# Windowed attention and a mixture of eight experts on one core: attention in steps ordered by shape, experts by 13 prepared widths, first slots of expert 0 beside routing

## The chip, the cores and the metric

The kernel runs on 1 core of a Trainium2 chip. The metric is device time in microseconds. All data are fp32. The engines are TensorE (PE; its weight loads stand apart as PEld), VectorE (DVE), ScalarE (ACT), GpSimd (POOL) and SyncE (SP); DMAs are issued from the queues of SP, ACT and POOL.

## The reference, cut to what matters

```python
# attention: q, k, v (4, 8, 768, 64); n_global = 8, n_local = 96
scores = q @ k.T / 8 - slope[h] * dist       # keep keys < n_global, and 0 <= i - j < n_local
a = softmax(scores);  x = (a @ v), heads side by side     # (3072, 512)
# router: 8 experts, one for each token
logits = (x / |x|) @ (emb / |emb|).T / tau
e = argmax(logits);  gate = softmax(logits)[e]
# expert e: w1[e] (512, 1024), w2[e] (1024, 512)
out[token] = gate * (relu(x[token] @ w1[e]) @ w2[e])
```

How many tokens an expert has depends on the data.

## The kernel before, in words

**Attention** (window_attention, L277). A group is one batch and four heads; there are 8. A group has 8 units (j = 0 to 7) of 96 keys and the first 30 rows as global keys; a unit's queries are the 192 columns from its first key on (96 for the last). For a unit TensorE computes scores (score, L337: four products of 64 rows by 126 by 192 columns), ScalarE takes exp (L341), VectorE multiplies by a table that holds bias and mask (L347), and one unit later TensorE adds the products with v (attend, L367, column pieces of 64) and the row sums (L373, column pieces of 32) in PSUM; a group's fourth and eighth unit close a half, which is copied out (L380, L382). Ahead of that, q and k are turned by transposes through `ident` (turn, L320). For every 128 tokens of a batch there follow: products with the normalised expert vectors `enb` (L405), transposes of the sums (L408) and of those products (L410), transposes of x (L430), a scaling by the reciprocal sum (L432), a store to `x_dram` and a sum of squares (L438).

**Routing** (choose, L145). Per batch, or per half of the last batch, VectorE finds the best expert as a one-hot `oh`; TensorE counts, by a product with the triangle `prefix` and one with `ones` (L171, L172), how many tokens of the same expert come earlier; VectorE adds the running count `cnt` and gets a slot; POOL scatters (token, gate) into that slot of `meta` (L199). Expert e owns slots e*3072 onwards.

**Experts** (load_rows L626, expert L648). For each expert SP reads the first 512 slots, POOL gathers four tiles of 128 rows of x (L640); empty slots point to a zero row. TensorE turns them (L655), VectorE copies (L656); 32 first products with 512 columns (L664), relu on ScalarE (L666); 32 second products, four tiles of 128 slots by 8 (L671); VectorE multiplies by the gate (L674), POOL scatters the rows to the output (L675). Every expert is computed at 512 slots. An unused tail (leftover, L681) handles more than 512 tokens of an expert and unusual n_global, n_local; all engines jump over it.

The order of the work on every engine comes from the framework's scheduler, which follows the order of the code and its priorities; waits between engines are semaphores. Weights alternate between two buffers.

## Time and profile before

| | us |
|---|---|
| median of 3 runs (lowest, highest) | 768.54 (766.0, 772.91) |
| the profiled execution | 777.63 |
| its span, first to last instruction | 775.8 |
| TensorE busy | 686.5 (88% of the span) |
| VectorE, ScalarE, POOL busy | 182.4, 147.6, 112.6 |
| mean granted TensorE clock | 0.95 |

The page has the span in 40 slices of 19.4 us; each digit is the busy share of a slice in tenths. PEclk is the granted clock, where 1.00 is 2.4 GHz and 0.50 is 1.2 GHz. In the chain of waits each step is the work that ended last. Idle time in brackets stands before a row, with what ended it. An fp32 product appears as two instructions in the trace, a transpose as one.

### The profile page before, as it was taken

What the parts mean: (1) busy time and instruction counts of PE and PEld (TensorE: products, weight loads), DVE (VectorE), ACT (ScalarE), POOL (GpSimd) and SP (SyncE); (2) the same over time, 40 slices, a digit from 0 to 9 for tenths busy, and PEclk for the clock granted to TensorE, in tenths of its full rate; (3) what the DMA queues carried; (4) which work ended last, traced back from release to release, by engine and by line L of the source; (5) the groups of instructions that cost most, each with busy time, mean ns of one, the idle gap of its engine ahead of it and who ended that gap; (6) DMA issues with size and microseconds to landing.
All of it is one profiled execution on the core that took longest, in us unless ns stands there. A gap on an engine that the chain in (4) does not pass through costs nothing.

```text
span 775.8 us, 8382 instructions
## 1 busy us (share of the span) xinstructions
PE 686.5 (88%) x3394; PEld 353.0 (46%) x3394; DVE 182.4 (24%) x500; ACT 147.6 (19%) x280; POOL 112.6 (15%) x131
## 2 busy tenths in 40 slices
PE   4989986989799519999999999999999999999992
PEld 2556654555465304444444444444444444444440
DVE  2435562664366601011011011011011011011010
ACT  3545532543453200100100100100100100100100
POOL 2110022013003232012012012012012011010010
PEclk9999989898999758999999999999999999999996
DMA  9977669650110922214214115115114114000000
GB/s 185 213 129 213 177 177 39 137 118 7 37 42 16 283 48 90 83 58 174 81 53 171 78 71 175 71 64 172 64 70 168 64 77 146 0 37 14 0 26 18
DMA packets 99898, 74.57 MB, mean 96 GB/s; under 512 B 80762, under 2 KB 80890, under 8 KB 99850
## 3 DMA queue, kind: packets, MB, share of 16 engines
q1 hardware_dynamic: 90538, 58.44, 29.8%
q0 software_dynamic: 5888, 14.71, 5.4%
q10 hardware_dynamic: 3424, 0.79, 0.6%
q8 instruction: 29, 0.48, 0.3%
q14 instruction: 19, 0.16, 0.1%
HBM read 61.11 MB, written 14.90 MB: 98 GB/s over the span
## 4 chain that ended last, share of the span: by engine, by line
PE 59%; DVE 4%; DMA 3%; issue 0%; POOL 0%; SPq 0%; ACT 0%; DVEq 0%; ACTq 0%
PE big L664 29%; PE work L671 28%; DVE xT L656 2%; DMA x_dram<-xs 1%; DMA xg<-x_dram,ids 1%; DMA meta<-mt,slot 1%; DVE y L674 1%; PE tp L405 0%; PE tp L430 0%; PE tp L408 0%; DMA emt<-meta 0%; PE od L367 0%; PE work L655 0%; POOL out_dram L675 0%; SPq L630 0%
## 5 line engine op out<-in xcount | busy, mean ns | idle before, releaser
L664 PE MATMUL big<-xT,w1t 128*128 128x512 f32 x512 | 224.0, 598 | 11.2 <-DVE xT L656 11.2
L671 PE MATMUL work<-w2t,hT 128*128 128x512 f32 x512 | 221.0, 592 | 0.0
L664 PEld LDWEIGHTS big<-xT,w1t 128*128 128x128 f32 x512 | 97.4, 192 | 133.2 <-issue 120.0
L671 PEld LDWEIGHTS work<-w2t,hT 128*128 128x128 f32 x512 | 97.3, 190 | 122.5 <-issue 122.5
L674 DVE TENSOR_SCALAR y<-work,emt 128x512 f32<-128x512 f32 x32 | 24.0, 751 | 387.2 <-PE work L671 387.2
L666 ACT ACTIVATE hT<-big 128x1024 f32<-128x1024 f32 x32 | 32.8, 1023 | 432.0 <-PE big L664 432.0
L347 DVE TENSOR_TENSOR ex<-ex,table 126x384 f32<-126x384 f32 (+1 forms) x128 | 70.1, 585 | 89.0 <-ACT ex L341 89.0
L675 POOL DMA_INDIRECT out_dram<-y,ids x32 | 31.8, 995 | 337.8 <-DVE y L674 330.1
L337 PE MATMUL sp<-qT,kT 64*126 64x192 f32 (+1 forms) x512 | 66.8, 364 | 7.9 <-ACT qT L325 5.8
L367 PE MATMUL od<-ex,v 126*64 126x192 f32 (+1 forms) x576 | 62.6, 320 | 8.6 <-issue 4.6
L341 ACT ACTIVATE ex<-sp 126x768 f32<-126x768 f32 x64 | 49.1, 767 | 82.6 <-PE sp L337 60.8
L337 PEld LDWEIGHTS sp<-qT,kT 64*126 64x126 f32 x512 | 43.9, 196 | 28.1 <-issue 13.1
L367 PEld LDWEIGHTS od<-ex,v 126*64 126x64 f32 x576 | 34.1, 138 | 28.5 <-issue 18.6
L640 POOL DMA_INDIRECT xg<-x_dram,ids x32 | 30.9, 966 | 85.4 <-issue 42.9
L373 PE MATMUL od<-ex,ones 126*32 126x192 f32 (+1 forms) x576 | 36.3, 321 | 0.0
L655 PE MATMUL work<-ident,xg 128*128 128x128 f32 x128 | 17.7, 293 | 18.9 <-DMA xg<-x_dram,ids 18.9
L199 POOL DMA_INDIRECT meta<-mt,slot x24 | 23.8, 993 | 44.1 <-DVE slot L190 30.3
L655 PEld LDWEIGHTS work<-ident,xg 128*128 128x128 f32 x128 | 15.5, 151 | 23.7 <-DMA xg<-x_dram,ids 20.1
L320 PE MATMUL tp<-ident,k 128*128 128x128 f32 x96 | 19.7, 329 | 6.3 <-DMA k<-in_k_dram 6.0
L311 POOL COPY v<-v 30x1792 f32<-30x1792 f32 x8 | 13.6, 1698 | 74.8 <-DMA v<-in_v_dram 46.6
L430 PE MATMUL tp<-ident,xd 128*128 128x128 f32 x96 | 16.3, 298 | 8.2 <-DVE lh L420 6.3
L656 DVE COPY xT<-work 128x512 f32<-128x512 f32 x32 | 20.1, 682 | 6.8 <-PE work L655 6.5
(113 smaller groups left out, 297.4 us busy)
## 6 DMA issues: line engine op xcount, KB each, us to landing
w1t<-in_moe_w_dram SPq DMA_DIRECT2D x8, 2048.0 KB, 7.9
w2t<-in_moe_w_dram SPq DMA_DIRECT2D x8, 2048.0 KB, 10.8
k<-in_k_dram SPq DMA_DIRECT2D x32, 192.0 KB, 3.5
v<-in_v_dram SPq DMA_DIRECT2D x32, 192.0 KB, 4.5
x_dram<-xs SPq DMA_DIRECT2D x24, 256.0 KB, 6.3
q<-in_q_dram SPq DMA_DIRECT2D x28, 192.0 KB, 3.9
q<-in_q_dram ACTq DMA_DIRECT2D x4, 192.0 KB, 6.1
xg<-x_dram,ids POOLq DMA_INDIRECT x32
```

The costliest lines, as they stand in the source:

```text
L337: nc.tensor.matmul(sp[0:ROWS, e, a * n : (a + 1) * n], lhsT=t.kT[rows, j, 0:ROWS], rhs=t.qT[rows, j * BLK : j * BLK + n], start=True, stop ...
L341: nc.scalar.activation(ex, sp[0:ROWS, :, 0 : 2 * n], AF.Exp, scale=k.scale)
L347: nc.vector.tensor_tensor(out=exv, in0=exv, in1=tb, op=ALU.mult)
L367: nc.tensor.matmul(od[a][e * D : (e + 1) * D, cols], lhsT=g.v[0:ROWS, 2 * a + e, j, :], rhs=ex[:, e, a * n + c0 : a * n + c1], start=first ...
L373: nc.tensor.matmul(od[2][32 * i : 32 * i + 32, cols], lhsT=k.ones[0:ROWS, 0:32], rhs=ex[:, e, a * n + c0 : a * n + c1], start=first, stop= ...
L655: nc.tensor.transpose(ps[:, c, :], xgs[j][:, c * P : (c + 1) * P], k.ident[:])
L656: nc.vector.tensor_copy(out=xT[:, :, j * P : (j + 1) * P], in_=ps[:])
L664: nc.tensor.matmul(ps[:, i, :], lhsT=w1[:, c, f * P : (f + 1) * P], rhs=xT[:, c, :], start=c == 0, stop=c == k.NC - 1)
L666: nc.scalar.activation(hT[:, 2 * f2 : 2 * f2 + 2, :], ps[:], AF.Relu)
L671: nc.tensor.matmul(ps[:], lhsT=hT[:, f, j * P : (j + 1) * P], rhs=w2[:, f, :], start=f == 0, stop=f == k.NF - 1)
L674: nc.vector.tensor_scalar_mul(y[:], ps[:], mt[:, j, 1:2])
L675: nc.gpsimd.indirect_dma_start(out=k.out[:, :], out_offset=bass.IndirectOffsetOnAxis(ap=ids[:, j : j + 1], axis=0), in_=y[:], in_offset=No ...
```

## The change

Attention now runs in 32 steps of two units (a fourth of a group); inside a step all scores come first, then transposes, then the products with v and the row sums of the step before. Exp is taken for one head parity at a time, the table is applied once for a unit. Sums of both groups of a batch share one tile (`halves`), so one transpose does for two. The choice is split into pieces that stand in later steps. The code's order is kept by `manual_schedule` on TensorE, ScalarE, VectorE and SP. The global rows of v come by DMA for every unit, not by a copy on POOL. Weights of expert 0 and 1 come in 32 pieces each, one at a time between other loads, both during the attention.

The last batch's halves are run so that its first half is routed early. After three batches the first 256 slots of expert 0 are gathered (first_rows), and their first products stand on TensorE around the last choice (first_product); the rest of expert 0 starts at the slot behind.

For every expert a width among 128, 160, ..., 512 is picked from its count (choose_widths). TensorE and ScalarE, and they alone, read it into a register (take_width) and jump into one of 13 prepared arms (Switch) that holds first products with that many columns, the next expert's transposes, second products of the full tiles but the first, and a remainder of 64 and 32 slots computed in two or four column pieces of the output (part_in_arm). The first tile's second products follow outside the arm (second). Each arm ends with a jump to the common end. A hint for the jump into the arm stands where the width is read, one for the jump out at the arm's start. Outputs of tiles that an arm doesn't compute have ids beyond the last row, which the scatter drops.

```diff
 CAP = 512
+PIECES = 32
+FIRST = 256
+WIDTHS = [128] + list(range(160, CAP + 1, 32))
...
-    nc.tensor.matmul(cp[:, 0:w], lhsT=k.prefix[:], rhs=ohf, start=True, stop=True)
-    nc.tensor.matmul(cp[:, w : 2 * w], lhsT=k.ones[:], rhs=ohf, start=True, stop=True)
+    nc.tensor.matmul(cp[:, 0:w], lhsT=k.prefix[:], rhs=oh.rearrange("p t e -> p (t e)"), start=True, stop=True,
+                     skip_group_check=True)
+    for t in range(n):
+        nc.tensor.matmul(cp[:, (t + 1) * E : w + E], lhsT=k.ones[:],
+                         rhs=oh[:, t : t + 1, :].to_broadcast([P, n - t, E]), start=False, stop=True,
+                         skip_group_check=True)
...
+    nc.vector.tensor_tensor(out=both, in0=cp[:, 0 : w + E].rearrange("p (t e) -> p t e", e=E),
+                            in1=k.cnt[:].unsqueeze(1).broadcast_to([P, n + 1, E]), op=ALU.add)
+    nc.vector.tensor_copy(out=k.cnt[:], in_=both[:, n, :])
...
         j, n = u.j, u.n
-        sp = sp_p.tile([P, 2, 512], F32, name="sp", tag="sp")
+        u.sp = [bank() for _ in range(2)]
+        u.ex = (late_p if u.late else ex_p).tile([P, 2, 2, 2 * BLK], F32, name="ex", tag="ex")
+        u.ex = u.ex[0:ROWS, :, :, 0:n]
         for a in range(2):
             t = u.g.pairs[a]
             for e in range(2):
                 rows = slice(e * D, (e + 1) * D)
-                nc.tensor.matmul(sp[0:ROWS, e, a * n : (a + 1) * n], lhsT=t.kT[rows, j, 0:ROWS],
+                nc.tensor.matmul(u.sp[e][0:ROWS, a * n : (a + 1) * n], lhsT=t.kT[rows, j, 0:ROWS],
                                  rhs=t.qT[rows, j * BLK : j * BLK + n], start=True, stop=True)
-        nc.scalar.activation(ex, sp[0:ROWS, :, 0 : 2 * n], AF.Exp, scale=k.scale)
-        kind = min(j, 2)
...
+    def grow(u, e):
+        nc.scalar.activation(u.ex[:, e], u.sp[e][0:ROWS, 0 : 2 * u.n].rearrange("p (a c) -> p a c", a=2), AF.Exp,
+                             scale=k.scale)
+    def weigh(u):
+        kind = min(u.j, 2)
+        tab = k.table[0:ROWS, u.g.m].rearrange("p e a i c -> p (e a) i c")[:, :, kind::(3 - kind), :]
+        exv = u.ex.rearrange("p e a (i c) -> p (e a) i c", c=BLK)
+        nc.vector.tensor_tensor(out=exv, in0=exv, in1=tab[:, :, 0 : u.n // BLK, :], op=ALU.mult)
...
+    def attend(g, p):
+        if p % 2 == 0:
+            g.od = [po_p.tile([P, 512], F32, name="od%d" % i, tag="od%d" % i) for i in range(3)]
+        parts = []
+        if p == 2:
+            parts.append((g.units[3], 0, BLK, 2 * BLK, True))
+        for j in (2 * p, 2 * p + 1):
+            parts.append((g.units[j], (j % QB) * BLK, 0, BLK if j % QB == QB - 1 else 2 * BLK, j == 0))
+        for u, at, c0, c1, first in parts:
             for a in range(2):
                 for e in range(2):
-                    nc.tensor.matmul(od[a][e * D : (e + 1) * D, cols], lhsT=g.v[0:ROWS, 2 * a + e, j, :],
-                                     rhs=ex[:, e, a * n + c0 : a * n + c1], start=first, stop=True,
+                    nc.tensor.matmul(g.od[a][e * D : (e + 1) * D, at : at + c1 - c0],
+                                     lhsT=g.v[0:ROWS, 2 * a + e, u.j, :],
+                                     rhs=u.ex[:, e, a, c0:c1], start=first, stop=True,
                                      skip_group_check=True)
+        for u, at, c0, c1, first in parts:
             for a in range(2):
                 for e in range(2):
                     i = 2 * a + e
-                    nc.tensor.matmul(od[2][32 * i : 32 * i + 32, cols], lhsT=k.ones[0:ROWS, 0:32],
-                                     rhs=ex[:, e, a * n + c0 : a * n + c1], start=first, stop=True,
+                    nc.tensor.matmul(g.od[2][32 * i : 32 * i + 32, at : at + c1 - c0], lhsT=k.halves[0:ROWS, g.m].rearrange("p i c -> p (i c)"),
+                                     rhs=u.ex[:, e, a, c0:c1], start=first, stop=True,
                                      skip_group_check=True)
...
+    def first_product(f):
+        if f % 2 == 0:
+            k.first.ps = bank()
+        ps = k.first.ps
+        for c in range(k.NC):
+            nc.tensor.matmul(ps[:, (f % 2) * FIRST : (f % 2 + 1) * FIRST], lhsT=k.w[0][0][:, c, f * P : (f + 1) * P],
+                             rhs=k.first.xT[:, c, :], start=c == 0, stop=c == k.NC - 1)
+        if f % 2:
+            nc.scalar.activation(k.first.hT[:, f - 1 : f + 1, :], ps[:].rearrange("p (i n) -> p i n", i=2), AF.Relu)
...
+        us = g.units[2 * p : 2 * p + 2]
+        for u in us:
             score(u)
-            if gi + 1 < len(groups):
-                turn(groups[gi + 1].pairs[u.j // 4], u.j % 4)
+        grow(us[0], 0)
+        grow(us[0], 1)
+        if s == 0:
+            next(table)
+        weigh(us[0])
+        grow(us[1], 0)
...
+        todo = [(x.pairs[a], i) for x, a, i in turns[s]]
+        if todo:
+            turn(*todo.pop(0))
+        grow(us[1], 1)
+        for x in todo:
+            turn(*x)
...
+        for hf in active:
+            half_turns(hf)
+        if s < len(steps) - 2:
+            weigh(us[1])
+        weights_part()
+        if s > 0:
+            q, qp = steps[s - 1]
+            attend(q, qp)
+            if q.m == 1 and qp % 2:
...
+    attend(*steps[-1])
+    for hf in active:
+        half_turns(hf)
+        half_router(hf)
+    hf = start_half(t, 1)
+    score_experts(hf, bank())
+    first_turn()
+    turn_sums(hf)
+    xs = [turn_x(t, 3)]
+    turn_products(hf)
+    next(hf.router)
+    xs += [turn_x(t, 4), turn_x(t, 5)]
+    for i in range(3):
+        store_x(t, 3 + i, xs[i])
+    weights_part(len(weights))
+    first_product(0)
+    hf.router.send(bank())
+    next(hf.router)
+    next(hf.router)
+    check_sums(t)
+    first_product(1)
+    for f in range(2, k.NF):
+        first_product(f)
...
+def turn_row(k, rows, xT, j, copy):
+    ps = k.work.tile([P, k.NC, P], F32, name="work", tag="work")
+    for c in range(k.NC):
+        k.nc.tensor.transpose(ps[:, c, :], rows[2][j][:, c * P : (c + 1) * P], k.ident[:])
+    copy(out=xT[:, :, j * P : (j + 1) * P], in_=ps[:])
...
+def second_in_arm(k, t, hT, w2, j):
+    nc = k.nc
+    ps = k.work.tile([P, k.DM], F32, name="work", tag="work")
+    for f in range(k.NF):
+        nc.tensor.matmul(ps[:], lhsT=hT[:, f, j * P : (j + 1) * P], rhs=w2[:, f, :],
+                         start=f == 0, stop=f == k.NF - 1)
+    nc.scalar.mul(t.y[:, j, :], ps[:], t.rows[0][:, j, 2:3])
+def part_in_arm(k, t, hT, w2, base, size):
+    nc, n = k.nc, P // size
+    m = k.DM // n
+    ps = k.work.tile([P, k.DM], F32, name="work", tag="work")
+    for f in range(k.NF):
+        for i in range(n):
+            nc.tensor.matmul(ps[i * size : (i + 1) * size, 0:m], lhsT=hT[:, f, base : base + size],
+                             rhs=w2[:, f, i * m : (i + 1) * m], start=f == 0, stop=f == k.NF - 1)
+    nc.scalar.mul(t.y_part[size][:], ps[:, 0:m], t.parts[size][1][:])
...
+def first_by_eight(k, xT, w1, hT, w, between=None):
+    nc = k.nc
+    for f in range(k.NF):
+        ps = k.big.tile([P, CAP], F32, name="big", tag="big")
         for c in range(k.NC):
+            nc.tensor.matmul(ps[:, 0:w], lhsT=w1[:, c, f * P : (f + 1) * P], rhs=xT[:, c, 0:w],
+                             start=c == 0, stop=c == k.NC - 1)
+        nc.scalar.activation(hT[:, f, 0:w], ps[:, 0:w], AF.Relu)
+        if between:
+            between(f)
...
+    if coming:
+        coming.xT = k.xtp.tile([P, k.NC, CAP], F32, name="xT", tag="xT")
+    def between(f):
+        for j in {5: (0,), 6: (1, 2), 7: (3,)}.get(f, ()) if coming else ():
+            turn_row(k, coming.rows, coming.xT, j, k.nc.scalar.copy)
+    tiles = range(0 if behind else 1, CAP // P)
+    for arm in tc.Switch(now.width.index, len(WIDTHS), hint=now.width.hint):
+        w = WIDTHS[arm]
+        first_by_eight(k, now.xT, w1, hT, w, between)
+        for size in (64, 32):
+            if w % (2 * size) >= size:
+                part_in_arm(k, now, hT, w2, w // (2 * size) * 2 * size, size)
+        for j in tiles:
+            if j < w // P:
+                second_in_arm(k, now, hT, w2, j)
+    if coming:
+        coming.width = take_width(k, coming.e)
+    def scatters():
+        for j in tiles:
+            scatter_rows(k, now.y[:, j, :], now.tile_ids[:, j : j + 1])
+        for size in (64, 32):
+            scatter_rows(k, now.y_part[size][:], now.parts[size][0][:], P // size)
+    out = [scatters]
+    if behind:
+        behind(out)
+    else:
+        second(k, now.rows, hT, w2, 0, k.work0, out)
+    return out
...
+def take_width(k, e):
+    t = Net()
+    v = k.nc.values_load(k.pick[0:1, e : e + 1], engines=ARMS, min_val=0, max_val=len(WIDTHS) - 1)
+    t.index, t.hint = {eng: v for eng in ARMS}, "expert%d" % e
+    k.tc.switch_hint(t.index, len(WIDTHS), t.hint)
+    return t
```

**TensorE in a step of the attention.** Left out are rows that only repeat. Before (sp and tp are PSUM tiles for scores and transposes, od for outputs and sums, xd and lS copies of them):

```order
L337 MATMUL sp<-qT,kT 126x192 x4
L320 MATMUL tp<-ident,q 128x128 x3
L430 MATMUL tp<-ident,xd 128x128 x4
L367 MATMUL od<-ex,v 64x192 x4
L373 MATMUL od<-ex,ones 32x192 x4
```

Now (pa stands for sp and tp, od_779 to od_781 for a group's od, halves for ones):

```order
L424 MATMUL pa<-qT,kT 126x192 x8
L405 MATMUL pa<-ident,k 128x128 x3
L405 MATMUL pa<-ident,q 128x128 x3
L522 MATMUL pa<-ident,xd 128x128 x4
L508 MATMUL pa<-ident,lS 128x128 x3
L450 MATMUL od_779<-ex,v 64x192 x2
L450 MATMUL od_780<-ex,v 64x192 x2
L450 MATMUL od_779<-ex,v 64x96 x2
L450 MATMUL od_780<-ex,v 64x96 x2
L458 MATMUL od_781<-ex,halves 32x192 x4
L458 MATMUL od_781<-ex,halves 32x96 x4
```

Scores come eight in a row, for two units, where there were four; products with v, and then row sums, come in eight (twelve in other steps) where there were four, and the pieces of od alternate.

**TensorE from the end of the attention to the first expert.** Before (oh is the one-hot choice, xg gathered rows, w1t and w2t an expert's weights, hT its relu):

```order
L430 MATMUL tp<-ident,xd 128x128 x4
L405 MATMUL tp<-xd,enb 32x128 x4
L408 MATMUL tp<-ident,xd 128x128 x2
L410 MATMUL tp<-ident,lS 128x128
L430 MATMUL tp<-ident,xd 128x128 x4
L410 MATMUL tp<-ident,lS 128x128
L171 MATMUL tp<-oh,prefix 128x24
L172 MATMUL tp<-oh,ones 128x24
L655 MATMUL work<-ident,xg 128x128 x16
L664 MATMUL big<-xT,w1t 128x512 x32
L671 MATMUL work<-w2t,hT 128x512 x32
```

Now (den is the tile of sums, fxT and fhT belong to the early 256 slots):

```order
L214 MATMUL pa<-oh,prefix 128x24
L217 MATMUL pa<-oh,ones 128x24
L217 MATMUL pa<-oh,ones 128x16
L217 MATMUL pa<-oh,ones 128x8
L603 MATMUL pa<-fxT,w1t 128x256 x28
L1121 TENSOR_LOAD pi
L1121 ISA x2
L1123 SWITCH_STRIDE
L1123 ISA
L1123 BRANCH_PREFETCH_HINT
L931 MATMUL work<-w2t,fhT 128x512 x8
L921 MATMUL work<-ident,xg 128x128 x16
```

Between the last choice and the first transposes of gathered rows, where nothing stood, there are 28 first products with 256 columns and 8 second products.

**TensorE in an expert.** Before, an expert is the last three rows of the last fence but one, eight times. Now, as it stands in the arm of 352 of expert 0:

```order
L1050 BRANCH_PREFETCH_HINT
L1029 MATMUL big<-xT,w1t 128x352 x24
L921 MATMUL work<-ident,xg 128x128 x4
L1029 MATMUL big<-xT,w1t 128x352 x4
L921 MATMUL work<-ident,xg 128x128 x8
L1029 MATMUL big<-xT,w1t 128x352 x4
L921 MATMUL work<-ident,xg 128x128 x4
L1011 MATMUL work<-w2t,hT 64x256 x16
L1011 MATMUL work<-w2t,hT 32x128 x32
L998 MATMUL work<-w2t,hT 128x512 x16
L1332 UNCONDITIONAL_BRANCH
```

The transposes (of the next expert's rows) stand between first products, and the remainder's products with 64 and 32 columns of weights ahead of the full tiles.

## Rows read from the trace of the kernel before

**Rows 1.** The page's slices of 19.4 us: TensorE, its clock, DMA rate.
```profile
PE   4989986989799519999999999999999999999992
...
PEclk9999989898999758999999999999999999999996
...
GB/s 185 213 129 213 177 177 39 137 118 7 37 42 16 283 48 90 83 58 174 81 53 171 78 71 175 71 64 172 64 70 168 64 77 146 0 37 14 0 26 18
```

**Rows 2.** Busy time by stage (windows): instructions in brackets; then clock, DMA share, GB/s.
```profile
100.00:200.00 100.00, 81.23 (x801) 50.03 (x801) 49.26 (x149) 38.58 (x85) 20.79 (x19) 0.89 0.57 84
256.00:294.00 38.00, 12.11 (x59) 8.66 (x59) 13.12 (x69) 2.94 (x10) 13.97 (x16) 0.56 0.55 177
...
414.00:472.00 58.00, 56.51 (x144) 25.86 (x143) 5.57 (x9) 4.09 (x4) 7.46 (x9) 1.00 0.28 104
```

**Rows 3.** The chain that ended last, experts: start us, us, engine, tile, line.
```profile
294.06 29.84 PE big L664 x64
...
471.48 27.73 PE big L664 x64
...
529.92 27.73 PE big L664 x64
...
732.97 27.48 PE work L671 x64
```

**Rows 4.** Timeline of TensorE from 125 to 131 us: start, us, line, shapes.
```profile
125.41 0.87 PE L367 MATMUL od<-ex,v 126*64 126x192 f32 x8
126.22 0.53 PE L373 MATMUL od<-ex,ones 126*32 126x192 f32 x8
126.68 0.68 PE L337 MATMUL sp<-qT,kT 64*126 64x96 f32 x8
127.29 0.55 PE L320 MATMUL tp<-ident,q 128*128 128x128 f32 x3
...
129.87 0.92 PE L337 MATMUL sp<-qT,kT 64*126 64x192 f32 x8
130.72 0.55 PE L320 MATMUL tp<-ident,k 128*128 128x128 f32 x3
```

**Rows 5.** The same from 86 to 88 us, products with 96 columns.
```profile
86.29 0.55 PE L367 MATMUL od<-ex,v 126*64 126x96 f32 x8
86.77 0.37 PE L373 MATMUL od<-ex,ones 126*32 126x96 f32 x8
87.07 0.39 PE L367 MATMUL od<-ex,v 126*64 126x96 f32 x4
```

**Rows 6.** The page's groups: transposes of gathered rows, busy us, mean ns.
```profile
L655 PE MATMUL work<-ident,xg 128*128 128x128 f32 x128 | 17.7, 293 | 18.9 <-DMA xg<-x_dram,ids 18.9
```

**Rows 7.** Timelines of POOL, ScalarE and TensorE in the first 26 us.
```profile
10.83 1.67 POOL L311 COPY v<-v 30x1792 f32<-30x1792 f32 x1 [9.13 <-DMA v<-in_v_dram]
17.49 3.41 ACT L274 ACTIVATE table<-rel 128x384 f32<-128x384 f32 x8 [3.85 <-DVE rel L270]
25.30 1.30 PE L367 MATMUL od<-ex,v 126*64 126x192 f32 x8
```

**Rows 8.** Timeline of TensorE around the choice of the first batch.
```profile
107.91 0.63 PE L171 MATMUL tp<-oh,prefix 128*128 128x48 f32 x2 [0.85 <-DVE oh L166]
...
111.19 1.65 PE L337 MATMUL sp<-qT,kT 64*126 64x192 f32 x8
```

**Rows 9.** Timeline of all engines from the last choice to the first expert.
```profile
269.06 0.59 PE L171 MATMUL tp<-oh,prefix 128*128 128x24 f32 x2 [4.25 <-DVE lg L177]
...
275.59 0.96 POOL L199 DMA_INDIRECT meta<-mt,slot  x1 [0.30 <-issue]
...
288.26 1.12 PE L655 MATMUL work<-ident,xg 128*128 128x128 f32 x4 [18.18 <-DMA xg<-x_dram,ids]
```

**Rows 10.** Control instructions behind the last product, by line: durations min/median/max in ns.
```profile
L699 PEldq TENSOR_LOAD <-fi x1: 492/492/492, 761.8 to 761.8; - x1
...
L700 PEldq COMPARE_BRANCH  x1: 4402/4402/4402, 762.4 to 762.4; - x1
```

More of the change, by code (lines that the diff above doesn't have):

```diff
@@ L41, in build_consts @@
     nc.vector.memset(k.ones[:], 1.0)
+    k.halves = pool.tile([P, 2, 2, 16], F32, name="halves")
+    nc.vector.memset(k.halves[:], 0.0)
+    for m in range(2):
+        nc.vector.memset(k.halves[:, m, m, :], 1.0)
 def build_route_consts(k):
@@ L178, in choose @@
     nc.scalar.activation(lg, lg, AF.Exp)
[L180 to L185 removed]
+    within = both[:, 0:n, :]
     nc.vector.tensor_tensor(out=within, in0=within, in1=oh, op=ALU.mult)
@@ L271, in window_table @@
     for m in range(2):
+        yield
         for e in range(2):
@@ L460, in window_attention @@
+    groups = [new_group(b, m) for b in range(B) for m in range(2)]
     for g in groups:
+        g.units = []
         for j in range(NB):
@@ new lines, in window_attention @@
+            g.units.append(u)
+    first = groups[0]
+    open_group(first)
+    numbers = load_numbers(k, k.n_global, k.n_local)
+    build_consts(k)
+    for a in range(2):
+        load_tokens(nc.sync, first.pairs[a].k, k.k, 0, a, 0, 3)
+        load_tokens(nc.scalar, first.pairs[a].q, k.q, 0, a, 0, 3)
+    next(numbers)
+    warm = const.tile([P, 1], F32, name="warm")
+    nc.scalar.activation(warm[:], k.ones[:, 0:1], AF.Exp)
+    for a in range(2):
+        load_tokens(nc.sync, first.pairs[a].q, k.q, 0, a, 3, NT)
@@ L478, in window_attention, with busy @@
+    for a in range(2):
+        load_tokens(nc.sync, first.pairs[a].k, k.k, 0, a, 3, NT)
+    idle = bank()
+    def busy(n):
+        for _ in range(n):
+            nc.tensor.matmul(idle[:, 0:64], lhsT=k.ones[:], rhs=k.ones[:, 0:64], start=True, stop=True)
+    busy(8)
+    load_v(first, range(4))
+    emb = prep_expert_emb(k, k.emb_in, k.tau, tmp)
+    next(emb)
+    open_group(groups[1])
+    for p in range(4):
+        load_part(groups[1], p)
     k.half = k.const.tile([P, NT], F32, name="half")
@@ L518, in window_attention @@
-    while tasks:
-        tasks.pop(0)()
+    table = window_table(k, tmp)
+    next(table)
+    next(numbers)
+    next(table)
+    check_numbers(k)
+    build_route_consts(k)
+    steps = [(g, p) for g in groups[: 2 * B - 2] for p in range(4)]
+    steps += [(g, p) for h in range(2) for g in groups[2 * B - 2 :] for p in (2 * h, 2 * h + 1)]
+    turns = [[] for _ in steps]
+    turn(first.pairs[0], 0)
+    turn(first.pairs[0], 2)
+    busy(3)
+    turn(first.pairs[1], 0)
+    turn(first.pairs[1], 2)
@@ new lines, in whole, with choose_widths @@
+def whole(k, rows, xT, w1, w2):
+    hT = k.hp.tile([P, k.NF, CAP], F32, name="hT", tag="hT")
+    first_by_eight(k, xT, w1, hT, CAP)
+    for j in range(CAP // P):
+        second(k, rows, hT, w2, j, k.work)
+def choose_widths(k):
+    nc, E, V = k.nc, k.E, len(WIDTHS)
+    over = k.const.tile([P, E, V - 1], F32, name="over")
+    k.need = k.const.tile([P, E], F32, name="need")
+    nc.vector.tensor_tensor(out=k.need[:], in0=k.cnt[:], in1=k.base[:], op=ALU.subtract)
+    nc.vector.tensor_tensor(out=over[:], in0=k.need[:].unsqueeze(2).broadcast_to([P, E, V - 1]),
+                            in1=k.wid[:].unsqueeze(1).broadcast_to([P, E, V - 1]), op=ALU.is_gt)
+    pick = k.const.tile([P, E], F32, name="pick")
+    nc.vector.reduce_sum(out=pick[:], in_=over[:], axis=AX.X)
+    k.pick = k.const.tile([P, E], I32, name="pi")
+    nc.vector.tensor_copy(out=k.pick[:], in_=pick[:])
+    split_widths(k, pick)
@@ new lines, with behind @@
+        with tc.manual_schedule(engines=ORDERED | set(ARMS) | {mybir.EngineType.Pool}):
+            choose_widths(n)
+            coming = numbers(0)
+            prepare(coming)
+            coming.width = take_width(n, 0)
+            second(n, n.first.rows, n.first.hT, n.w[0][1], 0, n.work)
+            coming.xT = n.xtp.tile([P, n.NC, CAP], F32, name="xT", tag="xT")
+            for j in range(CAP // P):
+                turn_row(n, coming.rows, coming.xT, j, nc.vector.tensor_copy)
+            split_rows(n, coming)
+            after, pending = numbers(1), []
+            split_rows(n, after)
+            for y, parts in ys:
+                for x in (y, *parts.values()):
+                    nc.vector.memset(x[:], 0.0)
+            for e in range(n.E):
+                now, coming, after = coming, after, None
+                if coming:
+                    prepare(coming)
+                for scatter in pending:
+                    scatter()
+                if e + 2 < n.E:
+                    after = numbers(e + 2)
+                    split_rows(n, after)
+                behind = None
+                if e == 0:
+                    def behind(out):
+                        second(n, n.first.rows, n.first.hT, n.w[0][1], 1, n.work0, out)
+                pending = expert(n, now, coming, behind)
+            for scatter in pending:
+                scatter()
```

693 lines of the change are left out of this document (428 added, 265 removed).

## The prediction, written before the changed kernel ran

> **What bounds the kernel now.** I read the page's slices first, then the chain of waits, then stages by window. The slices [rows 1] show two halves: up to about 290 us TensorE is busy in 5 to 9 tenths of a slice, from there on in 9 or more. The chain says why the second half has no slack: it is TensorE from 294.06 to 760.45, in eight equal periods of 58.4 us (471.48 to 529.92) [rows 3], each 27.73 us of first products and 27.48 us of second, the rest 16 transposes and a wait for their copies. Granted clock there 1.00 [rows 2]. So this half is bound by the columns that TensorE is given: a product with 512 columns stands as two instructions of 0.433 us. The first half is bound by order: between 100 and 200 us TensorE is busy 81.2 us and its clock is 0.89; between 256 and 294 us busy 12.1 of 38, clock 0.56 [rows 2].
>
> **Experts.** Before, every expert runs 512 slots, whatever it has. The reference's own formulas on its inputs give 406, 310, 510, 319, 322, 369, 472, 364 tokens; expert 0 has 315 of its tokens in the first three batches, so 256 slots go early and 150 remain. The thirteen widths then give 160, 320, 512, 320, 352, 384, 480, 384, together 2912.
> - First products: 27.73 x 2912/512 = **157.7 us** against 8 x 27.73 = 221.8.
> - Second products, full tiles of 128 slots: 1+2+4+2+2+3+3+3 = 20, and one of expert 0's early two: 21 x 27.48/4 = **144.3 us** [rows 3].
> - Remainders: four experts have a tile of 64 slots, three one of 32. Such a tile is computed in two or four column pieces side by side in the array. The nearest rows are the attention's products with 64 and 32 columns of weights: eight with 64 take 0.81 us for 192 columns and 0.48 for 96, eight with 32 take 0.46 and 0.30 [rows 4, 5], start to start. That is 0.43 and 0.21 ns per instruction and column, and 0.15 us fixed. A 64-tile is 32 instructions x 256 columns x 0.43 = 3.5 us, a 32-tile 64 x 128 x 0.21 = 1.7; with the fixed part 4 x 3.7 + 3 x 1.9 = **20 us**. Were nothing shared, each would cost a full tile, 6.87 us, 48 in all: +28 is the end above.
> - Transposes now stand between first products, their copies on ScalarE, beside products already queued: 7 x 16 x 0.138 = **15.5 us** [rows 6]; the first expert's remain ahead of its arm, as before.
> - Eight register loads on TensorE, 0.49 us each [rows 10], taken in full: **4 us**. The jumps into the arm and out of it I take as hidden: each hint stands 7 us of second products, or a whole arm, ahead of its jump.
>
> Sum 341.5 against 466.4: **-125 us**. Beside it: POOL issues at most ten indirect DMAs per expert at 0.96 us and 0.3 between [rows 9], 13 us against at least 26 of TensorE; ScalarE's copies and scalings are two or three a period. The 4.2 MB of expert 2's weights have expert 1's 36 us, 117 GB/s, and slices with such loads show 171 to 175 [rows 1].
>
> **Attention.** What the new order removes from TensorE is the fixed part of a group of like products. Eight score instructions take 0.85 us at 192 columns, 0.61 at 96 [rows 4], so 0.37 is fixed; of the two groups that follow them, 0.15 and 0.14 [rows 4, 5]. Groups fall from 64 to 32 for scores and from 72 to 32 for each of the others: 32 x 0.37 + 40 x 0.29 = 23.4 us. 24 transposes of sums go (3.3), 20 small counting products come, about 0.2 each at full clock (0.63 from start to end at the lowered one, [rows 8]): +4. **-23.** Ends: if the fixed part is a wait that moves along, 0; no excess beyond -26.
>
> **Start.** The first weighted product stands at 25.30 us [rows 7]. It waits for the table, whose exponentials start at 17.49 because POOL, ahead of the table's ramps, sat 9.13 us for a load of v before a copy. That copy is gone (a DMA writes those rows), all ramps follow each other, and four exponentials instead of eight come first. Without POOL's 9.1 us and half of ScalarE's 3.4 the product stands at about 14.5: **-11.** Ends -5 (the first 40 us move 185 to 213 GB/s, and v's rows add 2 MB in all) and -13.
>
> **Routing inside attention.** Before, a batch's choice stops TensorE (idle 0.85 us right before the counting product), and afterwards the eight scores that take 0.92 us take 1.65 [rows 4, 8]: the clock has dropped. Two choices fall between 100 and 200 us; of the 18.8 us idle there [rows 2] I give them 3 each, as much again to slow products, and 1 to the third choice. In the new order the counting products stand a step behind what they wait for. **-13**, ends 0 and -16.
>
> **Last choice to first arm.** Counting at 269.06, last scatter of slots issued at 275.59, rows arriving at 288.26, first product at 294.06 [rows 3, 9]: 25 us that a chain of DMAs sets. It stays. Into it go seven eighths of the early 256 slots' first products (27.73/2 x 7/8 = 12.1 us) and one of their two tiles (6.9): 19 of 25, so they cost nothing; uncovered, they would cost 19. Ahead of the choice, the work at clock 0.56 [rows 2] now has products among it: **-7**, ends 0 and -12.
>
> **Sum.** -125-23-11-13-7 = -179 us. The profiled execution took 777.63 us, span 775.8; the 15.3 us after the last product stay. 598.6 for that execution, which lies 9.1 above the median of the runs, 768.54: **590 us**.
>
> **A row that speaks against it.** Eight times two jumps are new. Before has one long jump of TensorE, over the unused tail: its branch took 4.40 us [rows 10]. Without cover, 16 of these are 70 us.
>
> The Trainium skill, page "Runtime: NRT & Kernel Launch", section "Instruction fetch mechanics", says that a taken branch whose target is not in the instruction window must have the target's page fetched before the engine goes on. The trace agrees with its 4.40 us. By that rule alone the sum would be 660, by hidden jumps 590.
>
> **Rivals.**
> - *Jumps exposed.* Price up to 16 x 4.40 = 70 us, 660; half of them 625. For it: the row above. Against it: a jump waits only for what is left of its fetch, and queued products run on meanwhile. Chance 0.14.
> - *Transfers bind the attention.* Up to the first arm the program now moves some 36 MB (before 30): 2 MB of v's rows and the second expert's 4.2 MB more, in less time, 175 GB/s over 205 us. The slices show 177 to 213 where loads press [rows 1], so there is little room. If attention ends where its transfers end, the -23 and half of -13 return: 615 to 620. Chance 0.13.
> - *Denser than I take it.* The old order loses more around its waits than I count; if TensorE runs the attention at nine tenths, another 20 to 30 us go: 562 to 570, or less. Chance 0.13.
> - *Widths don't take.* If every expert took the arm of 512, the first products are 64 us longer and the second ones, 33 tiles for 21 and remainders, 62: 716. Chance 0.02.
> - *Slower.* The clock stays at its lower level (1.2 GHz of 2.4) through the arms, because each begins with a stall: the 337 us of products would be 675, the time 927. It decides at 53% of the arms: 179 of 337 us at half rate eat the whole gain. Against it: after the 18 us of idle at 288.26 the first 64 products took 29.84 us and not 27.73 [rows 3, 9], so the clock came back within a few us. Chance 0.02.
>
> The forecast's own case has 0.56. **Range 560 to 640**: it leaves out about 0.07 below and 0.11 above (most of the jumps' case beyond half, widths, slower). Runs of before span 766 to 772.9, so about 1% is what can be told from no change. Faster by over 1%: 0.97; within: 0.01; slower: 0.02.
>
> **What would show each step.** First products: L1029's rows with 160 to 512 columns, 0.135 to 0.433 us apiece. Remainders: L1011's groups at 3.5 and 1.7 us; 6.9 means no sharing. Jumps: gaps of TensorE between the end of L931 and the first L1029, above 1 us if exposed. Attention: scores in groups of 16, first L450 near 14 us, no dip of the clock at the choices. Routing: first arm at 235 to 245 us, TensorE busy between choice and arm. Wrong it would be, above all, if the arms' first products wait for rows or weights, or if the attention's end doesn't come before 215 us.

## The result, and the profile after

The changed kernel took **588.94 us** (median of 4 runs, 587.84 to 590.12); the kernel before, beside it, 769.87 (766.0 to 772.91). The ratio is 0.765, 95% interval 0.761 to 0.769. The profiled execution took 587.84 us, span 585.9.

First the page's slices of the changed kernel, 14.6 us each: TensorE, its granted clock in tenths, GB/s.

```profile
PE   7899999999898998999999999999999999999930
...
PEclk9699999999989898999999999999999999999975
...
GB/s 174 195 180 204 251 245 177 241 244 92 55 127 173 139 69 96 235 163 93 203 136 33 38 232 134 232 157 56 207 149 91 180 152 11 1 54 18 2 39 18
```

Against [rows 1] the long row of 8s and 9s begins at about 30 us and not at 290, and in the first nine slices (132 us) the transfers run at 174 to 251 GB/s. The stages by window, from the first weighted product to the last choice, from there to the first arm, and the experts (columns as in [rows 2]):

```profile
21.51:197.66 176.15, 168.90 (x2075) 133.13 (x2074) 108.13 (x251) 102.08 (x269) 32.75 (x39) 0.97 0.79 175
197.66:223.40 25.74, 22.19 (x97) 15.96 (x96) 7.09 (x35) 3.80 (x9) 8.72 (x9) 1.00 0.50 133
223.40:561.00 337.60, 336.54 (x1282) 184.89 (x1282) 40.61 (x206) 57.32 (x112) 71.42 (x74) 1.00 0.35 116
```

The first of these stages in the kernel before, between the same two points:

```profile
25.30:269.06 243.76, 213.10 (x2193) 133.32 (x2191) 127.97 (x390) 103.67 (x224) 39.53 (x41) 0.93 0.56 118
```

TensorE has 44 us less to do there and 23 us less idle time (7.3 for 30.7). From the last choice to the first expert, where [rows 9] had one wait of 18.18 us, the timeline now reads:

```profile
197.66 0.81 PE L217 MATMUL pa<-oh,ones 128*128 128x24 f32 x6
198.33 12.33 PE L603 MATMUL pa<-fxT,w1t 128*128 128x256 f32 x56
...
210.50 7.03 PE L931 MATMUL work<-w2t,fhT 128*128 128x512 f32 x16
...
219.38 0.63 PE L921 MATMUL work<-ident,xg 128*128 128x128 f32 x4 [1.42 <-DMA xg<-x_dram,ids]
...
223.40 8.39 PE L1029 MATMUL big<-xT,w1t 128*128 128x160 f32 x48 [0.37 <-issue]
```

The way from choice to arm is as long as it was (25.7 for 25.0 us), now filled by the early slots of expert 0. The experts' products by shape (busy us, mean ns):

```profile
L1029 PE MATMUL big<-xT,w1t 128*128 128x384 f32 x128 | 41.9, 486 | 0.0
L1029 PE MATMUL big<-xT,w1t 128*128 128x320 f32 x128 | 35.4, 432 | 0.0
L1029 PE MATMUL big<-xT,w1t 128*128 128x512 f32 x64 | 28.0, 592 | 0.0
...
L1011 PE MATMUL work<-w2t,hT 128*64 128x256 f32 x128 | 14.7, 382 | 0.0
...
L1029 PE MATMUL big<-xT,w1t 128*128 128x160 f32 x64 | 10.9, 334 | 0.4 <-issue 0.4
L1011 PE MATMUL work<-w2t,hT 128*32 128x128 f32 x192 | 5.9, 274 | 0.0
```

The times of neighbours overlap, so busy time over the count is what one costs: 0.33 us with 384 columns, 0.28 with 320, 0.17 with 160. The last figure is a mixture. The first arm, the one of 160, begins while the granted clock is at 0.50 (1.2 GHz); here are its first 3.4 us and the 5 us that follow:

```profile
223.40:226.80 3.40, 3.40 (x13) 3.40 (x14) 3.01 (x18) 0.30 (x1) 0.00 (x0) 0.51 0.02 5
226.80:231.80 5.00, 5.00 (x37) 4.75 (x35) 4.45 (x27) 1.22 (x4) 2.84 (x3) 1.00 0.29 68
```

Thirteen products take 3.4 us at the lower level, 0.26 us each; at the full clock 37 take 5.0 us, 0.135 each. The end of the program, on POOL and VectorE:

```profile
555.09 0.98 POOL L1017 DMA_INDIRECT out_dram<-y_arm,tids  x1 [26.19 <-ACT y_arm L1000]
...
561.00 0.75 DVE L934 TENSOR_SCALAR y<-work,emt 128x512 f32<-128x512 f32 x1 [40.49 <-PE work L931]
...
570.43 0.98 POOL L1017 DMA_INDIRECT out_dram<-y,ids  x1 [2.54 <-DMA out_dram<-y,pids]
```

The last row of output is ready at 561.75 us and is sent at 570.43, because each of the last expert's six scatters waits until the one before has landed. From the last product to the span's end it is 24.9 us, before 15.3.

### The profile page after: what moved, and what is told of

Its sections match the earlier page's. It is cut to its first block, busy times and chain, and to the rows that moved or that the text cites. A ratio compares the mean times of both kernels' runs of the same rounds, so it can differ in the third digit from the quotient of the medians.

```text
span 585.9 us, 9204 instructions
## 1 busy us (share of the span) xinstructions
PE 544.4 (93%) x3542; PEld 348.2 (59%) x3542; DVE 165.7 (28%) x520; ACT 175.1 (30%) x416; POOL 120.9 (21%) x152
## 5 line engine op out<-in xcount | busy, mean ns | idle before, releaser
L1029 PE MATMUL big<-xT,w1t 128*128 128x320 f32 (+5 forms) x512 | 161.9, 473 | 0.4 <-issue 0.4
L1029 PEld LDWEIGHTS big<-xT,w1t 128*128 128x128 f32 x512 | 94.6, 194 | 61.4 <-issue 30.1
L998 PE MATMUL work<-w2t,hT 128*128 128x512 f32 x208 | 91.1, 595 | 0.0
L1031 ACT ACTIVATE hT<-big 128x320 f32<-128x320 f32 (+5 forms) x64 | 30.4, 474 | 185.1 <-PE big L1029 185.1
L435 DVE TENSOR_TENSOR ex<-ex,table 126x768 f32<-126x768 f32 x64 | 57.6, 904 | 56.7 <-ACT ex L428 54.9
L998 PEld LDWEIGHTS work<-w2t,hT 128*128 128x128 f32 x208 | 38.9, 190 | 47.6 <-issue 46.2
L428 ACT ACTIVATE ex<-pa 126x384 f32<-126x384 f32 (+1 forms) x128 | 53.3, 475 | 28.4 <-PE pa L424 28.4
L1017 POOL DMA_INDIRECT out_dram<-y_arm,tids x25 | 24.9, 997 | 174.9 <-ACT y_arm L1000 103.3
L424 PE MATMUL pa<-qT,kT 64*126 64x192 f32 (+1 forms) x512 | 49.8, 332 | 2.0 <-ACT ex L428 2.0
L931 PE MATMUL work<-w2t,hT 128*128 128x512 f32 x112 | 49.2, 592 | 0.0
L424 PEld LDWEIGHTS pa<-qT,kT 64*126 64x126 f32 x512 | 40.6, 187 | 12.5 <-issue 4.9
L931 PEld LDWEIGHTS work<-w2t,hT 128*128 128x128 f32 x112 | 21.3, 190 | 26.8 <-issue 26.8
L458 PE MATMUL od<-ex,halves 126*32 126x192 f32 (+1 forms) x576 | 27.4, 314 | 0.0
```

The costliest lines, as they stand in the source:

```text
L424: nc.tensor.matmul(u.sp[e][0:ROWS, a * n : (a + 1) * n], lhsT=t.kT[rows, j, 0:ROWS], rhs=t.qT[rows, j * BLK : j * BLK + n], start=True, st ...
L428: nc.scalar.activation(u.ex[:, e], u.sp[e][0:ROWS, 0 : 2 * u.n].rearrange("p (a c) -> p a c", a=2), AF.Exp, scale=k.scale)
L435: nc.vector.tensor_tensor(out=exv, in0=exv, in1=tab[:, :, 0 : u.n // BLK, :], op=ALU.mult)
L458: nc.tensor.matmul(g.od[2][32 * i : 32 * i + 32, at : at + c1 - c0], lhsT=k.halves[0:ROWS, g.m].rearrange("p i c -> p (i c)"), rhs=u.ex[:, ...
L931: nc.tensor.matmul(ps[:], lhsT=hT[:, f, j * P : (j + 1) * P], rhs=w2[:, f, :], start=f == 0, stop=f == k.NF - 1)
L998: nc.tensor.matmul(ps[:], lhsT=hT[:, f, j * P : (j + 1) * P], rhs=w2[:, f, :], start=f == 0, stop=f == k.NF - 1)
```

## The experiments

The kernels ran on three chips: e1 to e4 on one, e5 to e7 with c1 on the second, e8 to e10 with c2 on the third. There the kernel before took 778.57, 779.57 and 779.45 us and the changed kernel, as the controls c1 and c2 on the second and third chip, 598.75 and 599.89: both some 10 us more than in the first comparison. On the first of these chips there is no control, and the kernel before spread widely there: four of its eleven runs took 769.9 to 771.85 us, as in the first comparison, the rest 775 to 783. So times below are read against a control of 599 to 600, not against 588.94; for e1 to e4 that control is from another chip, and their own profiles carry the argument.

**e1: every expert takes the arm of 512.**

```diff
-    nc.gpsimd.iota(k.wid[:], pattern=[[WIDTHS[-1] - WIDTHS[-2], len(WIDTHS) - 1]], base=WIDTHS[0],
+    nc.gpsimd.iota(k.wid[:], pattern=[[WIDTHS[-1] - WIDTHS[-2], len(WIDTHS) - 1]], base=-CAP,
```

> All eight experts take the arm of 512, whatever they have; attention, routing and tail are those of the change. If the widths give back what columns and tiles say: first products 8 x 27.73 = 221.8 us for the 161.9 measured with the change (+60), second products 33 full tiles of 6.87 us for 21 and 20.6 us of remainders (+62): about 711 us. Rival: the experts' 129 us came at least half from elsewhere (no wait at an expert's edge, transposes between products): then at most 650 us.

Measured 724.2 us. The stretch from the first arm to the last product, in the control c1 and in e1:

```profile
233.26:571.08 337.82, 336.85 (x1283) 185.12 (x1282) 41.33 (x206) 57.22 (x112) 71.42 (x73) 0.99 0.34 116
236.18:697.28 461.10, 461.10 (x1154) 209.94 (x1154) 40.40 (x204) 68.86 (x117) 71.52 (x74) 1.00 0.25 85
```

That is 461.1 us for 337.8: +123.3, expected +121.7. Nearly all of the experts' gain is columns and tiles; hardly any of it is left for edges and waits.

**e2: widths in steps of 128 only.** (`pattern=[[P, CAP // P - 1], [0, 4]], base=P` in the same line, so the index is 0, 4, 8 or 12.)

> Only the widths 128, 256, 384 and 512 are chosen, so no expert has a remainder of 64 or 32 slots. If a remainder costs its share of the array: first products 27.73 x 3200/512 = 173.3 for 161.9 us (+11), 26 full tiles for 21 and 20.6 us of remainders (+14): about 614 us. Rival: pieces side by side save nothing against a full tile of 6.87 us: 5 full tiles more for 7 remainders at 6.87 us each, so second products fall by 14 and the time is 586 us or less.

Measured 624.91 us. The same stretch in e2:

```profile
233.00:597.77 364.77, 364.77 (x1043) 189.05 (x1042) 41.08 (x205) 59.18 (x110) 71.39 (x73) 1.00 0.32 107
```

It is 27.0 us longer than the control's, expected +25. The remainders do cost only their share (14.7 and 5.9 us in the rows above), so the pieces run side by side, and the narrow widths pay.

**e3: no hints ahead of the jumps into the arms.** (The hint at each arm's start, L1050, for the jump out of it, still stands in this kernel: TensorE's trace has it eight times. So the second half of the expectation, the way out, was not put to the test.)

```diff
-    k.tc.switch_hint(t.index, len(WIDTHS), t.hint)
...
-    for arm in tc.Switch(now.width.index, len(WIDTHS), hint=now.width.hint):
+    for arm in tc.Switch(now.width.index, len(WIDTHS)):
```

> The same arms, without the hints ahead of the jumps. If the hints hide the jumps: a wait of up to 4.2 to 4.4 us on TensorE at the way into each arm (8 x 4.3 = 34, 622 us), and as much at the way out of it (16 x 4.3 = 69, 657 us). Rival: the products queued ahead of a jump hide it without any hint: 588 us, gaps before the arm's first product under 1 us.

Measured 602.12 us, 2.2 and 3.4 above the controls of the other chips. TensorE, first arm of this kernel, and then the branches of TensorE's sequencer: the one into the first arm and all others, in e3 (L1331) and in c1 (L1332; number, then min/median/max in ns):

```profile
239.56 8.60 PE L1029 MATMUL big<-xT,w1t 128*128 128x160 f32 x48 [3.00 <-DVE high L978]
```

```profile
L1331 PEldq COMPARE_BRANCH  x1: 3517/3517/3517, 235.8 to 235.8; - x1
L1331 PEldq COMPARE_BRANCH  x15: 314/2072/7168, 256.4 to 562.6; - x15
L1332 PEldq COMPARE_BRANCH  x1: 453/453/453, 232.5 to 232.5; - x1
L1332 PEldq COMPARE_BRANCH  x15: 307/2839/6481, 249.2 to 556.3; - x15
```

The gap of 3.0 us is the one of its kind; behind it arms follow without one (337.8 us from there to the last product, as with hints). The row names VectorE, but the branch into this arm took 3.5 us where it took 0.45 with a hint: the gap is the jump. Ahead of it TensorE had waited for each tile of rows; ahead of the other arms there is a row of products without a gap, and there the branches take as long with hints as without, up to 6.5 and 7.2 us, while TensorE works on what is queued.

**e5: groups of eight again in the attention.**

```diff
-        for u in us:
-            score(u)
+        score(us[0])
...
-        grow(us[1], 0)
...
             turn(*todo.pop(0))
+        score(us[1])
+        grow(us[1], 0)
         grow(us[1], 1)
...
-        for u, at, c0, c1, first in parts:
             for a in range(2):
```

(The last loop is that of the row sums; without its head the sums of a unit come right behind its products.)

> The attention's products in groups of eight again (scores of one unit, a transposition, scores of the other; weighted products and sums alternating unit by unit), all else as in the change. If a group of like products has a fixed part (0.37 us for scores, 0.15 and 0.14 for the two that follow): 32 x 0.37 + 40 x 0.29 = 23 us more than the control, about 612 us by the change's 589. Rival: the fixed part is a wait that moves along, or the order matters for the idle time only: at most 5 us more.

Measured 609.51 us, 10.8 above the control on its chip. TensorE between first weighted product and last choice, in the control and in e5, and then a stretch of e5's timeline:

```profile
20.46:206.60 186.14, 171.18 (x2074) 134.08 (x2074) 107.47 (x250) 101.68 (x267) 31.48 (x39) 0.95 0.74 166
21.65:217.07 195.42, 189.17 (x2074) 125.66 (x2074) 107.47 (x249) 102.78 (x266) 33.17 (x39) 0.97 0.72 157
```

```profile
66.33 0.87 PE L450 MATMUL od<-ex,v 126*64 126x192 f32 x8
67.13 0.53 PE L457 MATMUL od<-ex,halves 126*32 126x192 f32 x8
67.60 0.87 PE L450 MATMUL od<-ex,v 126*64 126x192 f32 x8
```

The same 2,074 instructions take 171.2 us of TensorE in the control and 189.2 in e5. Counted in TensorE's order from the start to the last choice, the control has 32 groups each of scores, weighted products and sums, e5 has 59, 72 and 72; 27 x 0.37 + 40 x 0.15 + 40 x 0.14 = 22 us by the prediction's fixed parts, 18.0 measured. So the fixed part is real. But only 9.3 us of it reach the last choice in these two profiles, since idle time falls from 15.0 to 6.3 us. More than half of that fall is not the edit's mechanism: the control stood 7.0 us in two stops that come up again under c1 and c2, e5 2.3 us in one.

```profile
L405 PE MATMUL pa<-ident,k 128*128 128x128 f32 x81 | 14.5, 296 | 7.4 <-issue 7.0 <-ACT ex L428 0.4
L405 PE MATMUL pa<-ident,k 128*128 128x128 f32 x81 | 15.1, 297 | 2.3 <-issue 2.3
```

Another 2.6 us is a wait for rows of `q` that the slower TensorE no longer meets. Neither theory's total was right.

**e6: the early slots' products behind the wait.** (The loop over `first_product` and `second(..., 0, ...)` moved behind the four `turn_row` of the first arm; their sums use a `big` tile.)

> Expert 0's first 256 slots are still turned beside the routing, but their first products and the first of their two second tiles come behind the rows of its arm, not into the wait for them. If that wait of 25 us is a chain of transfers which products don't lengthen: 12 to 14 us of first products and 6.9 us of second ones more than the control, 19 to 21 us (about 609 us), with TensorE idle in the wait. Rival: the products take the clock, the weights' ports or the queues from that chain: without them it shortens, and less than 12 us are lost. On the other side, TensorE comes to the arm at its lower clock after 20 us of idle: up to 5 us more.

Measured 620.98 us, 22.2 above the control. TensorE after the choice:

```profile
228.45 1.08 PE L918 MATMUL work<-ident,xg 128*128 128x128 f32 x4 [20.55 <-DMA xg<-x_dram,ids]
...
234.00 15.73 PE L603 MATMUL big<-fxT,w1t 128*128 128x256 f32 x64
```

The rows come no earlier without those products (21.4 us behind the last choice, 20.7 in the control), so they cost nothing in the wait. Behind 20 us of idle time the granted clock is 0.50 from 228 to 234 us (1.2 GHz), four transposes take 1.08 us (0.63 above), and the clock is 1.00 again from 238 us on.

**e7: the second group's transposes one step later.** (`at = [2, 2, 2, 2, 3, 3, 3, 3]` for `[1, 1, 1, 2, 2, 2, 3, 3]`.)

> The transpositions of the second group of heads, which in the change stand ahead of the first weighted product and wait for their rows until 20 us, come one step later. If that wait is what holds the first weighted product at 21.5 us: it starts at 16 to 18 us, and the time falls by 2 to 4 us against the control. Rival: the first 40 us are bound by transfers or by the clock, which is at its lower level from 15 to 25 us: no more than 1 us.

Measured 599.66 us, 0.9 above the control. TensorE in e7, and one row of the control:

```profile
17.68 2.31 PE L450 MATMUL od<-ex,v 126*64 126x192 f32 x16
...
37.01 0.87 PE L405 MATMUL pa<-ident,q 128*128 128x128 f32 x3 [1.14 <-DMA q<-in_q_dram]
37.81 2.19 PE L450 MATMUL od<-ex,v 126*64 126x192 f32 x16
```

```profile
37.49 0.52 PE L405 MATMUL pa<-ident,q 128*128 128x128 f32 x3 [2.57 <-DMA q<-in_q_dram]
```

The first weighted product does come 2.8 us earlier than the control's (17.68 for 20.46). But both kernels wait for rows of `q` at 37 us, and the weighted products behind that wait start at 37.81 us in e7 and at 37.94 in the control: the lead is gone. So the first 37 us are bound by transfers. Behind the wait e7 runs some us at the lower clock (0.73 on average between 40 and 46 us, 1.00 in the control) and loses more.

**c1, c2: controls. e9: expert weights loaded later.** (`if s >= 16` for `if s >= 6`, and five pieces for three in the last steps.)

> The changed kernel as it is, as the control for the runs beside it. Expected: a ratio to the kernel before of 0.765, its first arm at 223 us and the end 25 us after the last product. Open: the four kernels run so far showed stops of 3 to 5 us near 94 and 143 us in which ScalarE, VectorE and TensorE stood together, and a first arm at 233 to 240 us; if the control shows them too, they belong to the execution and not to the edits.

> The changed kernel once more, as the control on this chip for the three runs beside it: a ratio of 0.765 to 0.768 to the kernel before. Whether the stops near 94 and 143 us, which the first profile of the change has not and five profiles on two other chips have, come here is open.

> The first two experts' weights are loaded in the steps from 16 of 32 on (about 118 us) and not from step 6 on (about 65 us), out of a stretch with 213 to 217 GB/s into one with 97 (140 to 200 us). If crowded transfers make the stops near 94 and 143 us: the first goes, the first arm comes 3 to 6 us earlier than the control's. Rival: the stops have another cause (an engine's own instructions, or the choice's scatters): no difference, within 2 us. On the other side: the weights come too late for the early first products at 195 us, which then wait, 5 us or more longer.

c1 took 598.75 us (0.768 of before), c2 599.89 (0.770), e9 600.76. The stops are in both controls; ScalarE in c1, and in e9:

```profile
94.60 0.87 ACT L428 ACTIVATE ex<-pa 126x384 f32<-126x384 f32 x2 [4.54 <-remote]
142.70 0.49 ACT L428 ACTIVATE ex<-pa 126x384 f32<-126x384 f32 x1 [4.60 <-remote]
```

```profile
92.38 0.49 ACT L428 ACTIVATE ex<-pa 126x384 f32<-126x384 f32 x1 [3.10 <-PE pa L405]
93.78 0.49 ACT L428 ACTIVATE ex<-pa 126x384 f32<-126x384 f32 x1 [0.92 <-PE pa L405]
95.25 0.33 ACT L428 ACTIVATE ex<-pa 126x192 f32<-126x192 f32 x1 [0.97 <-remote]
144.16 1.09 ACT L428 ACTIVATE ex<-pa 126x384 f32<-126x384 f32 x3 [5.37 <-remote]
```

So the stops don't come from the edits. Moving the weights removes neither: at the first, e9's three waits add up to 5.0 us, and the time doesn't fall. The view calls the releaser "remote" where it can't name one. But in all these rows, and in the kernel before, the semaphore that ScalarE waits for is one that in the trace only TensorE's instructions raise, and two rows of e9 name TensorE. TensorE in c1 during the two stops:

```profile
91.79:95.15 3.36, 0.00 (x1) 0.01 (x1) 0.56 (x1) 0.55 (x2) 2.52 (x3) 0.78 0.89 156
139.60:143.25 3.65, 0.01 (x2) 0.01 (x1) 0.56 (x1) 0.49 (x1) 2.69 (x3) 0.76 0.07 9
```

It is TensorE that stands, and ScalarE and VectorE stand behind it. Its last products are signalled late: in c1 the last of the scores starts at 91.04 us, and the signal that lets ScalarE go comes at 94.58. The first profile of the change was busy without a break between 91.79 and 95.15 us. In the second stop the DMAs move 9 GB/s: crowded transfers are not its cause.

**e4, e8: scatters that don't wait for one another; e10: with e9's edit.**

```diff
-    k.nc.gpsimd.indirect_dma_start(
+    i = k.nc.gpsimd.indirect_dma_start(
...
+    if k.free:
+        if k.outs:
+            k.tc.declare_no_dep(i.ins, group="outs", reason="rows are distinct")
+        k.tc.add_to_no_dep_group("outs", i.ins)
+        k.outs.append(i.ins)
```

> The scatters of the output rows no longer wait for one another (their rows are distinct). In the change's tail each of the last expert's six scatters is issued 2.3 to 3.6 us after the one before, when that one has landed, and the last at 570.43, 9.4 us after the last product's end (561.0). If that wait is what makes the tail longer than before's: scatters 1.3 us apart, the last one at about 562, 8 us less: 580 us. Rival: the queue of POOL takes one such transfer at a time whatever is declared: 588 us.

> The kernel whose output scatters don't wait for one another, again, now beside a control. Its tail was 18.8 us after the last product where the control of the second chip has 25.4: if that is the edit's, the time is 6 us (1%) below the control here. Rival: within 2 us of the control, the tail's gain being given back elsewhere.

> Both edits together: if each holds, 9 to 12 us below the control; if only the scatters' holds, 6.

(`k.free` is set to False ahead of `leftover`.) e4, without a control on its chip, took 593.18 us: 0.764 of before, from which nothing follows by itself. e8 took **592.77** (590.72 to 594.85) where the control beside it takes 599.89 (598.47 to 605.77): 7.1 us less, 0.760 of before (0.757 to 0.763) for 0.770 (0.767 to 0.774). e10 took 593.61: the scatters' part alone. POOL at e8's end:

```profile
571.79 0.98 POOL L1017 DMA_INDIRECT out_dram<-y,pids  x1 [0.30 <-issue]
573.08 0.98 POOL L1017 DMA_INDIRECT out_dram<-y,pids  x1 [0.31 <-issue]
574.86 0.98 POOL L1017 DMA_INDIRECT out_dram<-y,ids  x1 [0.80 <-DVE y L934]
```

1.29 us apart, and the last follows its row by 0.3 us. The tail falls from 24.9 us in c2 to 19.3, so it gives 5.6 of the 7.1 us. This is the fastest of the versions tried beside a control: 1.2% below it, with intervals that don't meet.

## Why the prediction was right, point by point

590 was foreseen, 588.94 came. The experts' mechanism and size were right; three other terms were mis-sized, and that their errors nearly cancel is luck. By terms, on the two profiled executions (spans 775.8 and 585.9, -189.9 where the sum had -179):

- **Experts: -125 foreseen, -128.8 measured** (466.4 to 337.6). First products 161.9 us busy for 157.7: 0.135 us apiece for 160 columns was right at the full clock, but the first arm begins with 3.4 us at 0.50, which cost 1.7 us; the rest is small excesses in every arm. Remainders 14.7 and 5.9 us for 4 x 3.7 and 3 x 1.9. The register loads that I charged with 4 us cost nothing: TensorE's idle time ahead of L1029 is 0.4 us in all. e1 and e2 confirm the mechanism to 2 us.
- **Rival "jumps exposed": did not happen**, and on the way into the arms needed the hints less than I thought: one gap of 3.0 us without them (e3). What the row of 4.40 us [rows 10] measures is a jump with nothing queued behind it. The Trainium skill, "Runtime: NRT & Kernel Launch", "Instruction fetch mechanics", has a taken branch whose target lies outside the instruction window stall the engine until the target's page is there; the first arm of e3 agrees with its 3.5 us, and where products are queued the runs show no such stall on TensorE. The way out of the arms was run with hints only.
- **Attention, routing and the work ahead of the last choice: -43 foreseen (23 + 13 + 7), -67.6 measured** (243.76 to 176.15): the step that was mis-sized. Two errors. The fixed parts were about right (e5), but I counted 64 and 72 groups before where TensorE's order has 75 of scores, 82 of weighted products and 73 of sums, for 32 each in the change: 43 x 0.37 + 50 x 0.15 + 41 x 0.14 = 29 us and not 23. Of the 44 us of busy time, fewer transposes and wider expert products did another 14 (L405, L408 and L410 took 29.4 us, L489, L498 and L508 take 15.1), less 5 for more counting products. The clock runs through all of these: the means of 0.93 and 0.97 stand for some 35 and 11 us at 0.50. And of the 18.8 us that TensorE stood idle between 100 and 200 us I left nearly 13 in place. ScalarE in the kernel before:

```profile
136.78 0.27 ACT L413 COPY lS<-tp 128x128 f32<-128x128 f32 x1 [8.31 <-remote]
...
188.34 0.81 ACT L341 ACTIVATE ex<-sp 126x768 f32<-126x768 f32 x1 [5.08 <-remote]
...
199.12 0.49 ACT L341 ACTIVATE ex<-sp 126x384 f32<-126x384 f32 x1 [5.62 <-remote]
```

  TensorE's waits of 6.26 us at 137.52, 1.79 at 189.20 and 4.02 at 198.83 fall into these three: stops like those of the controls. The changed kernel's first profile has none, so these 12 us went too, and not by the new order. They are near the 10.9 by which the sum fell short, and near the 9.1 by which the profiled execution of before lay above its median; subtracting those 9.1 is what kept the predicted median right. That the 9.1 us are the stops was not shown. Where the changed kernel has such stops, in c1, the same stretch takes 186.1 us and not 176.2. The sign "no dip of the clock at the choices" did not hold at the third: TensorE waited 2.2 us for `oh` from 158 us on, and 3.4 us at 0.50 followed.
- **Start: -11 foreseen, -3.8 measured** (25.30 to 21.51). The step that failed: I removed POOL's wait and half of ScalarE's table and took the product to follow. Late next were rows: the second group's transposes stand ahead of it and waited for `q` until 20.06 us, and e7 shows that without them transfers set the pace at 37 us.
- **Last choice to first arm: 0 foreseen, +0.7 measured** (25.0 to 25.7; 26.7 and 29.9 in the controls), its filling worth 19 foreseen, 22.2 in e6 with the lower clock behind the idle wait. The first arm came at 223.4 us, not 235 to 245, for the attention's sake.
- **Tail: 0 foreseen, +9.6 measured** (15.3 to 24.9). The step that failed: I carried over the old tail, in which one scatter follows each tile. In an arm the scatters come after all its products, six in a row, each behind the landing of the one before. e8 takes 5.6 us of it back.
- **"Transfers bind the attention"**: not as a whole (TensorE is busy 118.1 of the 118.5 us up to 140), but in the first 37 us (e7). **"Denser"** was the nearest rival: the attention's term came out at its size, though about half of the excess is the stops and not the old order, and the tail and the start took two thirds of it back. **"Slower"**: the clock's row stays at 9 through the arms, but for 3.4 us at the start of the first.
- **A reading of [rows 1]**: the slices up to 290 us stand not only at 5 to 9; the first has a 4, and the one behind the last choice a 1. No term rests on it.

So the total hides three misses: -24.6 in the attention against +7.2 at the start and +9.6 in the tail.

## What to carry to other kernels

Count groups of like products in the trace, not in the loops: a scheduler had cut them finer than the code. Before a slow figure is put down to a shape, look at the granted clock of the stretch that it comes from. When work moves into a branch, look at what now comes behind it in one burst, and whether the pieces of that burst wait for each other. Before a wait is charged to a step or carried over, read the engine that it waits for: if that one stood still for no reason that the profile shows, look at the same place in another execution, because the wait may belong to the execution and not to the code.

## What the runs showed of the hardware

- TensorE stops in places for some us with its last products signalled late, and ScalarE and VectorE stand behind it. ScalarE's waits there are 3.1 to 8.3 us, often with a releaser that the profile calls only "remote": four in the first 250 us of the kernel before's profile, none in the changed kernel's first profile, two there in each control's. In c1 the granted clock falls to 0.50 during each and stays there for 6.8 us (from 93.7 and 141.5 us).
- In both controls the two stops begin during the scatters of a choice on POOL (c1: 87.3 to 94.9 and 135.6 to 142.9 us). But the changed kernel's first profile has the same scatters and no stop, and in the kernel before the stop that ends at 136.78 begins after the last scatter was issued at 122.2. Moved weights don't remove them (e9). What causes them stays open.
- Both kernels took 10 us more in most of the later runs, on three chips, than in the first comparison. That the stops are this difference fits the changed kernel's stretch of 186.1 for 176.2 us (7.0 us of it idle in the two stops), but wasn't tested.
- Remainder tiles in two or four column pieces, side by side in the array, take 3.7 and 2.0 us where a full tile takes 6.87.
- A jump of TensorE into an arm takes 3.5 us where nothing is queued and no hint stands ahead of it, 0.45 with a hint, and no time of TensorE's where products are queued, with or without one (e3).
